# A weight's sign through an activation's slope, in an attention and two-MLP kernel with float64 weights

## The chip, the cores and the metric

The kernel runs on one core of a Trainium2 chip. The metric is the device time of one execution in microseconds (us). A difference under 0.2% is not told from none here.

## The reference, cut to what matters

```python
# q, k, v: [2, 12, 448, 64] float32; moe_w_in, moe2_w_in: [768, 2048], moe_w_out, moe2_w_out: [2048, 768], float64
scores = np.where(mask, -1e9, (q @ k.T) / 8)          # causal, per batch and head
attn = exp(scores - max); attn /= attn.sum(-1) + 1e-9
x = attn @ v                                          # reshaped to [896, 768]
h = np.maximum(x @ w_in, 0);  x = (h * h) @ w_out     # first MLP
h = x @ w_in2;  return (h - np.tanh(h)) @ w_out2      # second MLP
```

The weights are drawn in float32 and divided by a double, so they arrive as float64. The kernel takes them as pairs of 32-bit words and makes float32 of them on the chip.

## The kernel before, in words

**Three matmuls for one product.** Each MLP product is summed from three matmuls (lines 372 to 374): high part times high part, high times low, low times high. So every weight block and every activation is split into a high part, rounded by ScalarE, and a low part, the difference that VectorE takes.

**A weight unit and its passes.** The four weight matrices make 64 units (`NU`) of 128 x 768 weights. A unit is loaded by SyncE into one of three buffers `raw` (`w_load`, line 98). Then `w_prep` (lines 108 to 141) makes floats of it, with passes over 768 columns:

- `w_exp` on ScalarE (line 105): the upper word, read as float32, is scaled by 2^-112, which moves the exponent of a double to that of a float.
- `shift` on VectorE (line 115): the lower word is shifted right by 29.
- `merge` on VectorE (line 120): upper word shifted left by 3, or lower word. This drops the sign.
- `sign` on VectorE (line 125): the upper word's sign bit is put into the result.
- the conversion on ScalarE (line 127), the high part of the unit in a ring of 8 buffers `w`.
- `split` on VectorE (lines 134, 136): the low part. It frees the unit's `raw` buffer, into which unit u+3 is then loaded.

**Who sets the order.** The order on each engine is the order in which the code is written; no scheduler moves it. The VectorE passes stand in a list `todo` (lines 158 to 164): shift of unit u, split of unit u-1, merge of u, sign of u. `one()` takes the next pass while a budget lasts; each pass costs its price in `w_prep`, and each stage adds a share to the budget (`SHARE_PAIR` and the others, lines 37 to 40). The ScalarE passes are put into a second list, `act_late`, and are issued at the next call of `late()`, which the loop, `merge`, `split` and `need` make (`need` is called ahead of each MLP matmul group).

**Attention.** The loop over s has 14 stages for 12 pairs of heads. Stage s computes the scores of pair s, the exponentials of s and s-1, and the transposes and value product of pair s-2. In each stage ScalarE copies four transposed banks out of PSUM (`tcopy`, line 331), two ahead of the score maxima of the second half and two behind. From stage 8 on TensorE also runs one group of the first MLP's first product per stage (`fill`), ScalarE applies relu (line 487), square (493) and rounding (382) to it, and VectorE takes its low part (385) at the start of the next stage. From stage 2 to 7 a stage takes one pass from `todo`; from stage 8 on it takes three ahead of the second score maxima and what the budget leaves behind them.

**The MLPs.** After the loop TensorE runs the two MLPs in halves, with the remaining units prepared beside it.

Of the kernel before, what the change touches and what calls it, by code (L numbers as in the profile page):

```python
# [14 lines left out]
AF = mybir.ActivationFunctionType  # L15
ALU = mybir.AluOpType
# [17 lines left out]

SHARE_PAIR = (800, 3300)
SHARE_LAST = 3300
SHARE_HIDDEN = (2400, 500)
SHARE_OUT = 4000  # L40

EARLY = 6

# [21 lines left out]
def body(ctx: ExitStack, tc: tile.TileContext, qT, kT, vL, w1, w2, w3, w4, out):  # L65
    nc = tc.nc
# [24 lines left out]
    def words(u):  # L91
        v = raws[u].bitcast(I32).rearrange("p (n two) -> p n two", two=2)
        return v[:, :, 0], v[:, :, 1]

    def w_load(u):
        if u < NU:
            raws[u] = sb.tile([P, UC], I64, tag="raw", bufs=3, name=f"raw{u}")
            nc.sync.dma_start(out=raws[u], in_=units[u])

    def w_exp(u):  # L100


        if u < NU:
            h = words(u)[1].bitcast(F32)
            nc.scalar.activation(h, h, AF.Copy, scale=2.0**-112)  # L105

    def w_prep(u):

        st = {}

        def shift():
            if u == 0:
                act_late.append(lambda: w_exp(0))
            st["lo"], st["hi"] = lo, hi = words(u)
            nc.vector.tensor_scalar(out=lo, in0=lo, scalar1=29, scalar2=None, op0=ALU.logical_shift_right)

        def merge():
            late()
            lo, hi = st["lo"], st["hi"]
            nc.vector.scalar_tensor_tensor(out=lo, in0=hi, scalar=3, in1=lo, op0=ALU.logical_shift_left, op1=ALU.bitwise_or)  # L120
            act_late.append(lambda: w_exp(u + 1))

        def sign():
            lo, hi = st["lo"], st["hi"]
            nc.vector.scalar_tensor_tensor(out=lo, in0=hi, scalar=-0x80000000, in1=lo, op0=ALU.bitwise_and, op1=ALU.bitwise_or)  # L125
            st["w"] = ring(u)
            act_late.append(lambda: nc.scalar.copy(out=st["w"][:, 0], in_=lo.bitcast(F32)))  # L127

        def split():

            late()
            w, f = st["w"], st["lo"].bitcast(F32)
            if u % 2:
                nc.vector.scalar_tensor_tensor(out=w[:, 1], in0=w[:, 0].bitcast(F32), scalar=-(1.0 - 2.0**-24), in1=f, op0=ALU.mult, op1=ALU.add)  # L134
            else:
                nc.vector.tensor_sub(out=w[:, 1], in0=f, in1=w[:, 0])  # L136
            parts[u] = w
            raws.pop(u)
            w_load(u + 3)

        return [(shift, 470), (merge, 870), (sign, 870), (split, 870)]

    act_late = []
    budget = [0]
# [4 lines left out]
    def ring(u):  # L149
        taken.append(u)  # L150
        return sb.tile([P, 2, UC], F32R, tag="w", bufs=RING, name=f"w{u}")
# [6 lines left out]
    todo = []  # L158
    last = []
    for u in range(NU):  # L160
        shift, merge, sign, split = w_prep(u)
        todo += [(*shift, u, False), *last, (*merge, u, False), (*sign, u, True)]
        last = [(*split, u, False)]
    todo += last

    def late():
        while act_late:
            act_late.pop(0)()
# [120 lines left out]
    def blocks(n, t):  # L289
        return [c for cs in step(n, t) for c in cs]  # L290
# [162 lines left out]
    def first(l, half, m, b):  # L453

        u = (2 * l + half) * 2 * HALF + m
        dst = gdst(l, half, m, b)
        h = hbank(f"h{u}_{b}")
        for _ in first_pieces(l, half, m, b, h):
            pass
        if b == 1:  # L460
            freed[0] = u + 1
        return lambda: (act1, act2)[l](h, dst)
# [38 lines left out]
    def second(l, half, m, b):  # L501
        u0 = (2 * l + half) * 2 * HALF + HALF
        o = hbank(f"o{u0}_{m}_{b}")
        group(o, lambda k: (u0 + (m * HALF + k) // UNIT, (m * HALF + k) % UNIT), HALF, lambda k: g[k, b])
        if b == 1:
            freed[0] = u0 + (m + 1) * HALF // UNIT
        if half == 0:
            if b == 0 and m % 3 == 0:
                t = sb.tile([P, 3, B, S], F32, tag=f"v{m // 3}", name=f"part{l}_{m}")
                for i in range(3):  # L510
                    part[m + i] = t[:, i]
            nc.scalar.copy(out=part[m][:, b], in_=o)
        else:
            p = part[m][:, b]
            if l == 0:
                nc.vector.tensor_add(out=p, in0=o, in1=p)
                if b == 0:
                    x[m] = sb.tile([P, 2, B, S], F32R, tag=f"x{m}", name=f"y{m}")
                hi_of((x[m][:, 0, b], x[m][:, 1, b]), p)
                late()  # L520
                one()
                lo_of((x[m][:, 0, b], x[m][:, 1, b]), p)
            else:

                cuts = 2 if (m, b) == (KD - 1, B - 1) else 1
                w = S // cuts
                for i in range(cuts):
                    c = slice(i * w, i * w + w)
                    nc.vector.tensor_add(out=p[:, c], in0=o[:, c], in1=p[:, c])
                    (nc.scalar if i < cuts - 1 else nc.sync).dma_start(out=out[m * P : m * P + P, b * S + i * w : b * S + i * w + w], in_=p[:, c])  # L530
# [3 lines left out]
    for s in range(NPAIR + 2):  # L534
# [3 lines left out]
        if ss:  # L538
            budget[0] = min(budget[0], 0) + (SHARE_PAIR[f] if s > 1 else 0)
            e0, e1 = blocks(s, 0)[::-1], blocks(s, 1)  # L540
        else:
            budget[0] = min(budget[0], 0) + SHARE_LAST
        if sp:
# [73 lines left out]
    for l in range(2):  # L617
        for half in range(2):
# [3 lines left out]
            for m, b in order:  # L622
                budget[0] = min(budget[0], 0) + (SHARE_HIDDEN[l] if l == 1 or m < HALF - 1 else 0)
                first(l, half, m, b)()
                pump()
            flush()
            for m in range(KD):
                for b in range(B):
                    budget[0] = min(budget[0], 0) + SHARE_OUT
                    second(l, half, m, b)  # L630
# [39 lines left out]
```

## Time and profile before

| what | value |
|---|---|
| median of 3 runs (559.53 to 559.81) | 559.62 us |
| span of the profiled execution, first to last instruction | 558.0 us |
| granted TensorE clock, mean | 0.997 |
| TensorE matmuls busy | 550.9 us (99%), x3134 |
| VectorE busy | 403.7 us (72%), x727 |
| ScalarE busy | 336.6 us (60%), x650 |
| HBM read and written | 58.59 MB and 2.75 MB |

The page gives the span of the profiled execution and no time around it; the median lies 1.62 us above that span. Engines are named PE (TensorE matmul), PEld (its weight load), DVE (VectorE), ACT (ScalarE), POOL (GpSimd), SP (SyncE). Busy time counts a matmul from its start to a modelled end, so an engine shown as busy may still wait between matmuls.

### The profile page before, as it was taken

The page shows a single profiled execution, that of the slowest core. Times are in us where ns is not written, and L with a number is a line of the kernel's source. Part 1 is how long each engine was busy: PE and PEld are TensorE (multiplying, and loading weights), DVE is VectorE, ACT ScalarE, POOL GpSimd, SP SyncE. Part 2 cuts the span into 40 slices and gives each one's busy share as a digit, 9 for nine tenths or more (in the row PEclk, how much of TensorE's full clock was granted, in tenths as well). Part 3 has the DMA queues.
Part 4 walks back from the last instruction along what each step waited for, and adds up shares of the span by engine and source line. Part 5 has one row for each costly group of instructions (what it writes and reads, how often), then busy time and mean ns, then how long its engine had stood idle before and what let it go on. Part 6 is the DMA issues. An engine that isn't in the chain of part 4 may idle for free.

```text
span 558.0 us, 8044 instructions
## 1 busy us (share of the span) xinstructions
PE 550.9 (99%) x3134; PEld 482.4 (86%) x3134; DVE 403.7 (72%) x727; ACT 336.6 (60%) x650; POOL 1.8 (0%) x11
## 2 busy tenths in 40 slices
PE   7999999999999999999999999999999999999997
PEld 3666776899999999999999999999999999999996
DVE  5899998688574346564758599998887599988611
ACT  4999998777443347765334287876555587864100
POOL 1000000000000000000000000000000000000000
PEclk9899999999999999999999999999999999999999
DMA  8743421345253234222315130111666301015211
GB/s 275 253 156 107 141 64 58 125 158 168 78 178 123 80 116 156 89 97 107 115 57 167 61 113 1 56 58 56 195 205 202 124 11 57 1 56 186 84 49 49
DMA packets 15525, 61.85 MB, mean 111 GB/s; under 512 B 1664, under 2 KB 6400, under 8 KB 15488
## 3 DMA queue, kind: packets, MB, share of 16 engines
q1 hardware_dynamic: 15200, 61.00, 33.1%
q8 instruction: 24, 0.39, 0.3%
q10 hardware_dynamic: 288, 0.34, 0.2%
q14 instruction: 13, 0.11, 0.1%
HBM read 58.59 MB, written 2.75 MB: 110 GB/s over the span
## 4 chain that ended last, share of the span: by engine, by line
PE 84%; DVE 12%; ACT 2%; DMA 1%; issue 0%; DVEq 0%; ACTq 0%
PE o L372 14%; PE o L373 14%; PE o L374 14%; PE h L372 13%; PE h L374 13%; PE h L373 13%; DVE st L298 4%; DVE p L319 3%; ACT p L307 1%; PE o L343 1%; PE t L325 1%; DVE raw L120 1%; DVE x L360 1%; DMA k<-kT 1%; DVE st L300 1%; PE s L278 1%
## 5 line engine op out<-in xcount | busy, mean ns | idle before, releaser
L372 PE MATMUL o<-g,w 128*128 128x448 f32 x384 | 140.4, 366 | 0.0
L373 PE MATMUL o<-g,w 128*128 128x448 f32 x384 | 140.4, 366 | 0.0
L374 PE MATMUL o<-g,w 128*128 128x448 f32 x384 | 140.1, 365 | 0.0
L372 PEld LDWEIGHTS o<-g,w 128*128 128x128 f32 x384 | 72.1, 188 | 6.1
L374 PEld LDWEIGHTS o<-g,w 128*128 128x128 f32 x384 | 72.1, 188 | 6.0
L373 PEld LDWEIGHTS o<-g,w 128*128 128x128 f32 x384 | 72.1, 188 | 5.8
L127 ACT CAST w<-raw 128x768 fp32r<-128x768 f32 x64 | 58.0, 906 | 30.7 <-DVE raw L125 30.6
L105 ACT ACTIVATE raw<-raw 128x768 f32<-128x768 f32 x64 | 59.2, 924 | 23.6 <-DMA raw<-w 23.6
L372 PE MATMUL h<-x,w 128*128 128x448 f32 x192 | 72.7, 379 | 0.0
L374 PE MATMUL h<-y,w 128*128 128x448 f32 x192 | 70.6, 368 | 0.0
L373 PE MATMUL h<-y,w 128*128 128x448 f32 x192 | 70.6, 367 | 0.0
L372 PE MATMUL h<-y,w 128*128 128x448 f32 x192 | 70.6, 367 | 0.0
L373 PE MATMUL h<-x,w 128*128 128x448 f32 x192 | 70.5, 367 | 0.0
L374 PE MATMUL h<-x,w 128*128 128x448 f32 x192 | 70.5, 367 | 0.0
L125 DVE SCALAR_TENSOR_TENSOR raw<-raw 128x768 int32<-128x768 int32 x64 | 61.2, 957 | 1.2
L120 DVE SCALAR_TENSOR_TENSOR raw<-raw 128x768 int32<-128x768 int32 x64 | 61.0, 953 | 0.0
L136 DVE TENSOR_TENSOR w<-raw,w 128x768 fp32r<-128x768 f32 x32 | 30.6, 957 | 31.2 <-ACT w L127 31.0
L307 ACT ACTIVATE p<-s,st 128x128 f32<-128x128 f32 (+6 forms) x84 | 39.7, 485 | 9.2 <-DVE st L300 9.2
L134 DVE SCALAR_TENSOR_TENSOR w<-w,raw 128x768 fp32r<-128x768 f32 x32 | 30.6, 958 | 18.5 <-ACT w L127 18.5
L385 DVE TENSOR_TENSOR g<-r,g 128x448 fp32r<-128x448 f32 x32 | 20.0, 624 | 31.0 <-ACT g L382 30.9
L372 PEld LDWEIGHTS h<-x,w 128*128 128x128 f32 x192 | 36.0, 188 | 4.1
L374 PEld LDWEIGHTS h<-y,w 128*128 128x128 f32 x192 | 36.0, 188 | 3.4
(59 smaller groups left out, 744.7 us busy)
## 6 DMA issues: line engine op xcount, KB each, us to landing
raw<-w SPq DMA_DIRECT2D x64, 768.0 KB, 4.3
q<-qT SPq DMA_DIRECT2D x12, 224.0 KB, 4.8
k<-kT SPq DMA_DIRECT2D x11, 224.0 KB, 3.8
out<-part SPq DMA_DIRECT2D x11, 224.0 KB, 1.9
v<-vL SPq DMA_DIRECT2D x2, 1152.0 KB, 6.8
vend<-vL SPq DMA_DIRECT2D x1, 384.0 KB, 10.0
k<-kT ACTq DMA_DIRECT2D x1, 224.0 KB, 3.6
out<-part ACTq DMA_DIRECT2D x1, 112.0 KB, 1.7
```

The costliest lines, as they stand in the source:

```text
L105: nc.scalar.activation(h, h, AF.Copy, scale=2.0**-112)
L120: nc.vector.scalar_tensor_tensor(out=lo, in0=hi, scalar=3, in1=lo, op0=ALU.logical_shift_left, op1=ALU.bitwise_or)
L125: nc.vector.scalar_tensor_tensor(out=lo, in0=hi, scalar=-0x80000000, in1=lo, op0=ALU.bitwise_and, op1=ALU.bitwise_or)
L127: act_late.append(lambda: nc.scalar.copy(out=st["w"][:, 0], in_=lo.bitcast(F32)))
L134: nc.vector.scalar_tensor_tensor(out=w[:, 1], in0=w[:, 0].bitcast(F32), scalar=-(1.0 - 2.0**-24), in1=f, op0=ALU.mult, op1=ALU.add)
L136: nc.vector.tensor_sub(out=w[:, 1], in0=f, in1=w[:, 0])
L298: nc.vector.tensor_reduce(out=st[:, 0, SI[c] : SI[c] + 1], in_=sc[n, c], axis=AX.X, op=ALU.max, negate=True)
L307: nc.scalar.activation(prob[n % 3][:, POFF[c] : POFF[c] + w], sc.pop((n, c)), AF.Exp, bias=st[:, 0, i : i + 1], scale=0.125, accum_out=st[ ...
L372: nc.tensor.matmul(h, lhsT=hi, rhs=xh, start=(k == 0), stop=False)
L373: nc.tensor.matmul(h, lhsT=hi, rhs=xl, start=False, stop=False)
L374: nc.tensor.matmul(h, lhsT=lo, rhs=xh, start=False, stop=(k == kk - 1))
L385: nc.vector.tensor_sub(out=dst[1], in0=v, in1=dst[0])
```

## The change

ScalarE's pass on the upper word becomes a parametric relu: a word that is not negative is scaled by 2^-112 as before, a negative one by 2^-112 times 2^32. The 32 that this adds to the exponent field is bit 28 of the word, and `merge` shifts it to bit 31, the sign's place. VectorE's `sign` is gone. The conversion of unit u is now queued by `merge` and stands ahead of `w_exp` of unit u+1. The shares are scaled by about 0.72, the new sum of a unit's prices over the old.

```diff
-SHARE_PAIR = (800, 3300)
-SHARE_LAST = 3300
-SHARE_HIDDEN = (2400, 500)
-SHARE_OUT = 4000
+SHARE_PAIR = (575, 2370)
+SHARE_LAST = 2370
+SHARE_HIDDEN = (1725, 360)
+SHARE_OUT = 2870
...
-            nc.scalar.activation(h, h, AF.Copy, scale=2.0**-112)
+            nc.scalar.activation(h, h, AF.Prelu, scale=2.0**-112, alpha=2.0**32)
...
             nc.vector.scalar_tensor_tensor(out=lo, in0=hi, scalar=3, in1=lo, op0=ALU.logical_shift_left, op1=ALU.bitwise_or)
-            act_late.append(lambda: w_exp(u + 1))
-
-        def sign():
-            lo, hi = st["lo"], st["hi"]
-            nc.vector.scalar_tensor_tensor(out=lo, in0=hi, scalar=-0x80000000, in1=lo, op0=ALU.bitwise_and, op1=ALU.bitwise_or)
             st["w"] = ring(u)
             act_late.append(lambda: nc.scalar.copy(out=st["w"][:, 0], in_=lo.bitcast(F32)))
+            act_late.append(lambda: w_exp(u + 1))
...
-        return [(shift, 470), (merge, 870), (sign, 870), (split, 870)]
+        return [(shift, 470), (merge, 870), (split, 870)]
...
-        todo += [(*shift, u, False), *last, (*merge, u, False), (*sign, u, True)]
+        todo += [(*shift, u, False), *last, (*merge, u, True)]
```

TensorE's own order is the same in both, and ScalarE's has one table load in both, ahead of the first exponential. In the changed kernel the lines behind `w_prep` have numbers lower by 4, and lines 127, 134 and 136 are 122, 130 and 132. Names carry the number of the pair or unit: st9 is the statistics of pair 9, raw3 and w3 belong to unit 3.

ScalarE in stage 9, from the exponential of 384 columns to the rounding of the MLP group, before:

```order
L307 ACTIVATE p0_122,st9_981<-s9_0_1_941,st9_981 128x384
L105 ACTIVATE raw4_870<-raw4_870 128x768
L331 COPY pt7_967<-t7_2_1016 128x512
L331 COPY pt7_967<-t7_3_1022 128x512
L307 ACTIVATE p0_122,st9_981<-s9_0_0_940,st9_981 128x448
L487 ACTIVATE r_1035<-h1_0_958 128x448
L307 ACTIVATE p0_122,st9_981<-s9_1_0_998,st9_981 128x256
L307 ACTIVATE p0_122,st9_981<-s9_1_0_998,st9_981 128x192
L307 ACTIVATE p0_122,st9_981<-s9_1_1_999,st9_981 128x320
L493 ACTIVATE r_1035<-r_1035 128x448
L382 CAST g0_0_0_0_830<-r_1035 128x448
L127 CAST w3_1049<-raw3_706 128x768
```

and now:

```order
L303 ACTIVATE p0_122,st9_978<-s9_0_1_938,st9_978 128x384
L122 CAST w3_995<-raw3_613 128x768
L105 ACTIVATE raw4_861<-raw4_861 128x768
L327 COPY pt7_964<-t7_2_1015 128x512
L327 COPY pt7_964<-t7_3_1021 128x512
L303 ACTIVATE p0_122,st9_978<-s9_0_0_937,st9_978 128x448
L483 ACTIVATE r_1034<-h1_0_955 128x448
L303 ACTIVATE p0_122,st9_978<-s9_1_0_996,st9_978 128x256
L303 ACTIVATE p0_122,st9_978<-s9_1_0_996,st9_978 128x192
L303 ACTIVATE p0_122,st9_978<-s9_1_1_997,st9_978 128x320
L489 ACTIVATE r_1034<-r_1034 128x448
L378 CAST g0_0_0_0_830<-r_1034 128x448
```

The conversion of unit 3 has moved from behind the rounding to a place ahead of the last two bank copies. Stages 8, 10 and 11 show the same, with units 2, 4 and 5.

VectorE from the low part at the head of stage 10 to the second score maxima of that stage, before:

```order
L385 TENSOR_TENSOR g0_0_0_0_830<-r_1035,g0_0_0_0_830 128x448
L115 TENSOR_SCALAR raw4_870<-raw4_870 128x768
L298 TENSOR_REDUCE st10_1103<-s10_0_1_1062 128x1 x2
L298 TENSOR_REDUCE st10_1103<-s10_0_0_1061 128x1
L300 TENSOR_SCALAR st10_1103<-st10_1103 128x3
L360 TENSOR_TENSOR x1_68<-o7_1050,x1_68 128x448
L134 SCALAR_TENSOR_TENSOR w3_1049<-w3_1049,raw3_706 128x768
L311 TENSOR_SCALAR st9_981<-st9_981 128x7
L312 RECIPROCAL st9_981<-st9_981 128x7
```

and now:

```order
L381 TENSOR_TENSOR g0_0_0_0_830<-r_1034,g0_0_0_0_830 128x448
L130 SCALAR_TENSOR_TENSOR w3_995<-w3_995,raw3_613 128x768
L294 TENSOR_REDUCE st10_1102<-s10_0_1_1059 128x1 x2
L294 TENSOR_REDUCE st10_1102<-s10_0_0_1058 128x1
L296 TENSOR_SCALAR st10_1102<-st10_1102 128x3
L356 TENSOR_TENSOR x1_68<-o7_1048,x1_68 128x448
L120 SCALAR_TENSOR_TENSOR raw4_861<-raw4_861 128x768
L307 TENSOR_SCALAR st9_978<-st9_978 128x7
L308 RECIPROCAL st9_978<-st9_978 128x7
```

The merge of unit 4 stands where the split of unit 3 stood, and the split where the shift stood. Stage 11 has the same order with units 4 and 5. In stage 9 the merge of unit 3 stands behind three more normalisations, at the place that it had before; in stage 8 the merge of unit 2 takes that place, where the split of unit 1 stood before.

## Rows read from the trace of the kernel before

**Rows 1.** Windows: stretch and length, busy us (instructions) per engine, granted clock, DMA.
```profile
70.23:79.88 9.65, 9.65 (x88) 7.21 (x86) 9.02 (x25) 8.84 (x25) 0.00 (x0) 1.00 0.26 79
107.00:554.50 447.50, 447.50 (x2193) 411.18 (x2191) 309.81 (x447) 244.07 (x387) 0.00 (x0) 1.00 0.31 101
```
**Rows 2.** Timeline of PE, first scores of stages 3, 6, 7, 8: start us, us.
```profile
20.27 0.59 PE L278 MATMUL s<-k,q 64*64 64x448 f32 x2
...
38.75 0.62 PE L278 MATMUL s<-k,q 64*64 64x448 f32 x2
...
44.62 0.59 PE L278 MATMUL s<-k,q 64*64 64x448 f32 x2
...
50.96 0.59 PE L278 MATMUL s<-k,q 64*64 64x448 f32 x2
```
**Rows 3.** Timeline of PE, a value product of stage 9 and transposes of stage 12.
```profile
68.47 1.84 PE L343 MATMUL o<-pt,v 128*64 128x448 f32 x12
...
93.93 1.14 PE L325 MATMUL t<-ident,p 128*128 128x128 f32 x8 [0.25 <-ACT pt L331]
```
**Rows 4.** Timeline of DVE, stages 8 to 11; in brackets idle time before, and its releaser.
```profile
57.29 0.95 DVE L134 SCALAR_TENSOR_TENSOR w<-w,raw 128x768 fp32r<-128x768 f32 x1
...
62.69 0.61 DVE L385 TENSOR_TENSOR g<-r,g 128x448 fp32r<-128x448 f32 x1
...
67.44 0.95 DVE L120 SCALAR_TENSOR_TENSOR raw<-raw 128x768 int32<-128x768 int32 x1
...
69.99 0.95 DVE L125 SCALAR_TENSOR_TENSOR raw<-raw 128x768 int32<-128x768 int32 x1
...
72.39 0.63 DVE L385 TENSOR_TENSOR g<-r,g 128x448 fp32r<-128x448 f32 x1 [0.49 <-ACT g L382]
...
75.26 0.95 DVE L134 SCALAR_TENSOR_TENSOR w<-w,raw 128x768 fp32r<-128x768 f32 x1
...
82.11 0.62 DVE L385 TENSOR_TENSOR g<-r,g 128x448 fp32r<-128x448 f32 x1 [0.50 <-ACT g L382]
```
**Rows 5.** Timeline of ACT, stage 9, and the conversion in stage 11 with its follower.
```profile
66.36 0.93 ACT L105 ACTIVATE raw<-raw 128x768 f32<-128x768 f32 x1
67.17 1.06 ACT L331 COPY pt<-t 128x512 f32<-128x512 f32 x2
68.12 0.65 ACT L307 ACTIVATE p<-s,st 128x448 f32<-128x448 f32 x1
...
68.74 0.55 ACT L487 ACTIVATE r<-h 128x448 f32<-128x448 f32 x1
69.82 0.47 ACT L307 ACTIVATE p<-s,st 128x256 f32<-128x256 f32 x1 [0.53 <-DVE st L300]
...
71.18 0.58 ACT L493 ACTIVATE r<-r 128x448 f32<-128x448 f32 x1
71.79 0.57 ACT L382 CAST g<-r 128x448 fp32r<-128x448 f32 x1
...
91.71 0.90 ACT L127 CAST w<-raw 128x768 fp32r<-128x768 f32 x1
92.51 0.36 ACT L307 ACTIVATE p<-s,st 128x128 f32<-128x128 f32 x1
```
**Rows 6.** Lines by form: line, engine, operation, shapes, count, busy us, mean ns, idle before.
```profile
L125 DVE SCALAR_TENSOR_TENSOR raw<-raw 128x768 int32<-128x768 int32 x64 | 61.2, 957 | 1.2
...
L115 DVE TENSOR_SCALAR raw<-raw 128x768 int32<-128x768 int32 x64 | 35.5, 555 | 0.0
...
L105 ACT ACTIVATE raw<-raw 128x768 f32<-128x768 f32 x64 | 59.2, 924 | 23.6 <-DMA raw<-w 23.6
L127 ACT CAST w<-raw 128x768 fp32r<-128x768 f32 x64 | 58.0, 906 | 30.7 <-DVE raw L125 30.6
...
L412 ACT ACTIVATE w<-u,abias 128x448 f32<-128x448 f32 x32 | 21.5, 671 | 1.0
```
**Rows 7.** Lines by form of ACT, the one table load.
```profile
L225 ACT ACT_TABLE_LOAD x1 | 1.3, 1283 | 1.2 <-PEq L663 1.2
```

More of the change, by code (lines that the diff above doesn't have):

```diff
@@ L160, in body @@
     for u in range(NU):
-        shift, merge, sign, split = w_prep(u)
-        todo += [(*shift, u, False), *last, (*merge, u, False), (*sign, u, True)]
+        shift, merge, split = w_prep(u)
+        todo += [(*shift, u, False), *last, (*merge, u, True)]
         last = [(*split, u, False)]
```

## The prediction

> **What bounds the kernel now.** I read the windows first, then the timelines of the three engines that hand work to each other in the attention stages, then the lines by form for the price of a pass. From 107.00 to 554.50 us TensorE is busy for the whole 447.5 us at full clock while VectorE works 309.8 us of it [rows 1]. There VectorE and ScalarE have room, and a pass less on VectorE moves nothing. So the change can act on the time only before 107 us, in the attention stages.
>
> There the reader should compare three clocks. **TensorE:** the stages without MLP work start at 20.27, 38.75, 44.62 and 50.96 us for stages 3, 6, 7 and 8 [rows 2]. The shortest of them, stage 6, takes 44.62 - 38.75 = 5.87 us. Five of these would take 29.35, and the five from 20.27 to 50.96 took 30.69, so TensorE loses 1.34 us there to waits. From stage 8 on a stage takes 9.65 us with TensorE busy throughout [rows 1]. **VectorE and ScalarE:** they go round a loop of nearly the same length. The low part of the MLP group (L385) starts at 62.69, 72.39 and 82.11 us, that is every 9.70 and 9.72 us, and each time VectorE has waited about 0.5 us for ScalarE's rounding [rows 4]. So in stages 9 to 11 two things are nearly tied: TensorE's own work, 9.65 us, and the loop from the low part through the score maxima, the exponentials, square and rounding back to the next low part, 9.7 us. A stage becomes longer as soon as that loop does.
>
> The pass that is removed, `sign`, stands at 69.99 us in stage 9 [rows 4]. That is behind the maxima for which ScalarE waited until 69.82 [rows 5], and VectorE still has to wait before 72.39. In these stages the sign pass lies in the shadow of ScalarE; it is not on the loop.
>
> **The change, part by part.**
>
> *The sign pass.* 64 passes of 0.957 us, 61.2 us of VectorE's time [rows 6]. All but the first nine or so run beside a TensorE that is never idle [rows 1]: nothing. Of the early ones, those of stages 8 to 11 lie in the shadow named above: nothing, as long as ScalarE closes the loop. What cover there is, is that wait of 0.5 us, and it grows below. Those of units 0 and 1 stand in stages 4 and 8. The places move up there, so that up to the merge of stage 8 VectorE has the passes shift 1, split 0, merge 1, shift 2, split 1 instead of sign 0, shift 1, split 0, merge 1, sign 1, shift 2: a pass of 0.957 less. Against it, ScalarE gets two passes in a row (a conversion and the next unit's exponent pass) in front of the exponentials of stages 4 and 7, 1.6 us by the price below, on which scores and VectorE's low part of x wait. I set the two against each other and let VectorE reach the place of the merge in stage 8 at 57.29 us as before [rows 4]; the bounds are 0.96 earlier and 0.7 (1.6 less 0.96, rounded up) later.
>
> *The slope.* The same 768 columns in place. The exponent pass takes 0.924 and the conversion 0.906 [rows 6]; the dearest activation with an extra operand takes 0.671 for 448 columns [rows 6], 1.15 for 768 if scaled. The bounds are 0.906 and 1.15; I take 0.924, since it is the same instruction with the same shape, 0.81 from its start to the next one's start (66.36 to 67.17) [rows 5].
>
> *The conversion's new place.* This is the term that decides. In stages 8 to 11 the conversion of the unit just merged now stands between the 384-column exponential and the last two bank copies, together with the exponent pass. That is a longer piece of ScalarE work there, and a wait: the conversion reads what `merge` writes, so ScalarE stands still until VectorE's merge is done. Before, only the exponent pass stood there, which needs no merge and ran at 66.36, while VectorE began the merge at 67.44 [rows 4, 5]. Behind the waiting conversion are queued: the exponent pass, two bank copies (for TensorE's value product, which started at 68.47 [rows 3]), the 448-column exponential, relu, three exponentials, square and rounding. VectorE's next low part waits for the rounding.
>
> The length of that ScalarE piece, start to start [rows 4, 5]: conversion 0.81 (taken as the exponent pass's), exponent pass 0.81, two copies 67.17 to 68.12 = 0.95, exponential 68.12 to 68.74 = 0.62, relu 0.55, three exponentials 69.82 to 71.18 = 1.36, square 71.18 to 71.79 = 0.61, rounding up to VectorE's start 71.79 to 72.39 = 0.60. The sum is **6.31 us**. The hand from VectorE to ScalarE costs 0.03.
>
> - Stage 8: merge at 57.29, done at 58.24, conversion at 58.27, the low part of stage 9 at 64.58: 1.89 late against 62.69 [rows 4].
> - Stage 9: from low part to merge 67.44 - 62.69 = 4.75, the order between is as before; merge 0.95, hand 0.03, ScalarE 6.31: a round of 12.04 instead of 9.70. Late by 4.23.
> - Stage 10: the merge stands where the split stood, 75.26 - 72.39 = 2.87 after the low part [rows 4], plus 0.40 since a split (0.957, as every pass of this form) stands where a shift of 0.555 stood [rows 6]: 3.27. With 0.95, 0.03 and 6.31 the round is 10.56 instead of 9.72. Late by 5.07.
> - Stage 11: the same order, late by 5.91.
>
> Then 0.80 comes back: the conversion that stood behind the rounding in stage 11 (91.71 to 92.51) [rows 5] is no longer ahead of the exponential and the bank copies for which TensorE waited at 93.93 [rows 3]. From there the order gives TensorE no other waiting than before, and it is full to the end. So 5.91 - 0.80 = **5.1 us** stay. TensorE shows them as waits ahead of the value products of stages 9 to 11 and the transposes of stage 12. The 1.34 us of earlier waits are not gained, because stage 12 starts by the loop and not by TensorE.
>
> *DMA.* The load of unit 3 is issued one stage earlier on SyncE's queue, ahead of the q of pair 9 and the k of pair 8; these are needed at stage 9 and 8, many us later. I cost it at nothing; were the k late, stage 8 would start late, and it is inside the bound of 0.7.
>
> *Shares.* They keep the passes at about the same place per unit; after 107 us it costs nothing.
>
> The sum is made against the profiled span of 558.0 us: 563.1. The median of the runs is 1.62 above that span, so I add 5.1 to 559.62: **564.7 us**.
>
> **The rivals.**
>
> *One turn only* (0.12). If stages 10 and 11 fall back to TensorE's 9.65, because VectorE's passes overlap more than I count, only 1.89 + 2.34 - 0.80 = 3.4 us stay: 563.0. For it: the merge is early in those stages. Against it: the round of 10.56 has no slack in the rows.
>
> *TensorE stays the bound: faster* (0.13). If the conversion never has to wait for the merge, ScalarE has nothing more to do per stage than before, and TensorE could run its stages back to back: 1.34 us gained, 558.3 us. It decides in favour of this if VectorE is more than 2 us ahead of today's place, so that the merge of stage 9 ends at 66.36 instead of 68.39, when ScalarE is free. For it: VectorE has a pass less per unit. Against it: VectorE cannot run ahead past the low part, which waits for ScalarE's rounding already now [rows 4].
>
> *Hidden anyway* (0.10). The longer piece in mid-stage is made up by the earlier start of the next stage's copies, and gains and losses cancel: 559.6 us.
>
> *The slope is dearer or not the same function set* (0.05). One table load is 1.283 us [rows 7], and the order of the changed kernel holds only that one. If the pass itself took twice the 0.924, the loop would get 0.92 more in four rounds, 3.7 us: 568.4. The Trainium skill ("ScalarE activation tables: per-element evaluation and per-set limits", What a function is on this engine) says that with the same operands an instruction costs the same whichever table it reads, and that functions of two sets are one table load apart. By its first half this rival falls away and the sum stays; by its second a set without the slope would put loads around every such pass. No row before shows this function.
>
> **How the numbers follow.** The forecast has 0.60, the rivals 0.12, 0.13, 0.10 and 0.05. The forecast's own range: relu may overlap its follower as the exponent pass does, 0.93 - 0.81 = 0.12 in each of four rounds (-0.5) [rows 5], and with -0.96 at stage 8's start this gives 563.3; +0.7 and a pass of 1.15 in four rounds (+0.9) give 566.3. The range that holds 8 in 10 takes in these, the one-turn case and the case of no change, and leaves out the faster and the dearest: 559.4 to 566.3. What 0.2% is, 1.1 us, is about what a measurement can tell from no change. Slower by more: 0.60 + 0.12 + 0.05 = 0.77. Within: 0.10. Faster: 0.13.
>
> **What would show it.** In the changed profile, right: the low part L381 of stages 9 to 11 comes every 12 and 10.5 us; ScalarE's conversions L122 there wait for VectorE's L120; VectorE's wait for the rounding grows from 0.5 to over 2 us; TensorE idles about 2 us in stage 9 and 0.8 in 10 and 11; the table load stays one. The forecast is wrong if the low parts keep their pitch of 9.7 us, if the conversions there wait for nothing, or if the time after the loop changes.

## The result, and the profile of the changed kernel

The changed kernel takes 564.40 us (median of 4 runs, 564.12 to 564.56), the kernel before, run beside it, 559.67 (559.53 to 559.81): a ratio of 1.0087, 95% interval 1.0074 to 1.0099, or 4.7 us slower. The forecast was 564.7. The profiled execution has a span of 562.8 us against 558.0, 4.8 more. Engines over the span, from the profile's first part:

```profile
PE 552.0 (98%) x3134; PEld 481.3 (86%) x3134; DVE 345.6 (61%) x663; ACT 333.9 (59%) x650; POOL 1.8 (0%) x11
```

VectorE has 64 instructions and 58 us less, and the kernel is slower: the engine's busy share was no guide. Two groups of the lines by form of ScalarE, the slope and the conversion, and a window behind the attention stages (columns as in rows 6 and 1):

```profile
L105 ACT ACTIVATE raw<-raw 128x768 f32<-128x768 f32 x64 | 59.2, 925 | 0.0
L122 ACT CAST w<-raw 128x768 fp32r<-128x768 f32 x64 | 57.8, 904 | 32.2 <-DVE raw L120 32.2
```
```profile
107.00:559.00 452.00, 452.00 (x2222) 414.33 (x2221) 258.80 (x392) 245.33 (x393) 0.00 (x0) 1.00 0.31 102
```

The slope costs what the scaling cost [rows 6], and from 107 us TensorE is busy throughout at full clock as before [rows 1]. So the time went ahead of that. The timeline of VectorE, merges (L120) and low parts (L381) of stages 8 to 12, to be laid beside [rows 4]:

```profile
57.38 0.95 DVE L120 SCALAR_TENSOR_TENSOR raw<-raw 128x768 int32<-128x768 int32 x1
...
64.54 0.62 DVE L381 TENSOR_TENSOR g<-r,g 128x448 fp32r<-128x448 f32 x1 [3.56 <-ACT g L378]
...
69.30 0.95 DVE L120 SCALAR_TENSOR_TENSOR raw<-raw 128x768 int32<-128x768 int32 x1
...
76.44 0.62 DVE L381 TENSOR_TENSOR g<-r,g 128x448 fp32r<-128x448 f32 x1 [3.08 <-ACT g L378]
...
79.71 0.95 DVE L120 SCALAR_TENSOR_TENSOR raw<-raw 128x768 int32<-128x768 int32 x1
...
86.92 0.62 DVE L381 TENSOR_TENSOR g<-r,g 128x448 fp32r<-128x448 f32 x1 [2.12 <-ACT g L378]
...
97.38 0.62 DVE L381 TENSOR_TENSOR g<-r,g 128x448 fp32r<-128x448 f32 x1 [2.10 <-ACT g L378]
```

The low part of stage 12 in the kernel before:

```profile
91.84 0.63 DVE L385 TENSOR_TENSOR g<-r,g 128x448 fp32r<-128x448 f32 x1 [0.50 <-ACT g L382]
```

The low parts come after 11.90, 10.48 and 10.46 us instead of 9.70 and 9.72, and VectorE's wait for the rounding (L378) has grown from 0.5 to between 2.1 and 3.6. What the rounding was late for stands in the timeline of ScalarE, stage 9 and the conversion of stage 10, against [rows 5]:

```profile
67.31 0.57 ACT L303 ACTIVATE p<-s,st 128x384 f32<-128x384 f32 x1
...
70.29 0.88 ACT L122 CAST w<-raw 128x768 fp32r<-128x768 f32 x1 [2.32 <-DVE raw L120]
71.08 0.88 ACT L105 ACTIVATE raw<-raw 128x768 f32<-128x768 f32 x1
71.86 1.05 ACT L327 COPY pt<-t 128x512 f32<-128x512 f32 x2
72.81 0.64 ACT L303 ACTIVATE p<-s,st 128x448 f32<-128x448 f32 x1
...
75.84 0.56 ACT L378 CAST g<-r 128x448 fp32r<-128x448 f32 x1
...
80.70 0.90 ACT L122 CAST w<-raw 128x768 fp32r<-128x768 f32 x1 [0.42 <-DVE raw L120]
```

ScalarE is free at 70.29 - 2.32 = 67.97, stands still for 2.32 us until VectorE's merge of 69.30 is done, and only then come the exponent pass and the bank copies, which could have run. The copies started at 67.17 before. TensorE waits for those copies; its timeline, first scores of stages 3 and 8, the value product of stage 9, and its waits up to the transposes of stage 12; below them, the last part of that value product in the kernel before:

```profile
19.94 0.59 PE L274 MATMUL s<-k,q 64*64 64x448 f32 x2
...
52.33 0.59 PE L274 MATMUL s<-k,q 64*64 64x448 f32 x1
...
69.84 0.97 PE L339 MATMUL o<-pt,v 128*64 128x448 f32 x4
72.48 1.08 PE L339 MATMUL o<-pt,v 128*64 128x320 f32 x8 [1.67 <-ACT pt L327]
73.49 0.27 PE L339 MATMUL o<-pt,vend 64*64 64x64 f32 x2
...
82.97 1.08 PE L339 MATMUL o<-pt,v 128*64 128x320 f32 x8 [0.63 <-ACT pt L327]
...
93.42 1.08 PE L339 MATMUL o<-pt,v 128*64 128x320 f32 x8 [0.58 <-ACT pt L327]
...
94.97 0.47 PE L368 MATMUL h<-x,w 128*128 128x448 f32 x1 [0.20 <-ACT r L483]
...
98.67 1.14 PE L321 MATMUL t<-ident,p 128*128 128x128 f32 x8
```
```profile
70.23 0.27 PE L343 MATMUL o<-pt,vend 64*64 64x64 f32 x2
```

These waits are 3.1 us. Before stage 8, from 19.94 to 52.33, the five stages take 32.39 us against 30.69 [rows 2], 1.7 more; since stage 3 starts 0.33 earlier than before, stage 8 starts 1.37 late. The transposes of stage 12 start at 98.67 instead of 93.93 [rows 3]: 4.74 of the 4.8 us are lost by then, 1.37 ahead of stage 8 and 3.37 behind its start. That is more than the waits alone, 3.1 less the old 0.25 [rows 3]. An interrupted value product loses more than the idle time in brackets: that of stage 9 takes 73.49 - 69.84 = 3.65 us up to its last part instead of 70.23 - 68.47 = 1.76 [rows 3], 1.89 more around a wait of 1.67.

### The profile page after: what moved, and what is told of

Read it like the earlier page. It is cut to its first block, busy times and chain, and to the rows that moved or that the text cites. A ratio compares the mean times of both kernels' runs of the same rounds, so it can differ in the third digit from the quotient of the medians.

```text
span 562.8 us, 8014 instructions
## 1 busy us (share of the span) xinstructions
PE 552.0 (98%) x3134; PEld 481.3 (86%) x3134; DVE 345.6 (61%) x663; ACT 333.9 (59%) x650; POOL 1.8 (0%) x11
## 4 chain that ended last, share of the span: by engine, by line
PE 83%; DVE 8%; ACT 7%; issue 1%; DMA 1%; DVEq 0%; ACTq 0%
PE o L368 14%; PE o L369 14%; PE o L370 14%; PE h L368 13%; PE h L370 13%; PE h L369 13%; ACT p L303 3%; DVE st L294 3%; DVE p L315 2%; ACT pt L327 1%; ACT raw L105 1%; PE t L321 1%; DVE x L356 1%; PE o L339 1%; DMA k<-kT 1%
## 5 line engine op out<-in xcount | busy, mean ns | idle before, releaser
L120 DVE SCALAR_TENSOR_TENSOR raw<-raw 128x768 int32<-128x768 int32 x64 | 61.0, 953 | 0.0
L381 DVE TENSOR_TENSOR g<-r,g 128x448 fp32r<-128x448 f32 x32 | 20.0, 625 | 57.5 <-ACT g L378 57.5
L132 DVE TENSOR_TENSOR w<-raw,w 128x768 fp32r<-128x768 f32 x32 | 30.6, 957 | 36.6 <-ACT w L122 36.4
L508 ACT COPY part<-o 128x448 f32<-128x448 f32 x24 | 12.8, 534 | 58.2 <-PE o L370 58.2
L130 DVE SCALAR_TENSOR_TENSOR w<-w,raw 128x768 fp32r<-128x768 f32 x32 | 30.6, 956 | 25.3 <-ACT w L122 25.2
L115 DVE TENSOR_SCALAR raw<-raw 128x768 int32<-128x768 int32 x64 | 35.6, 557 | 5.6 <-DMA raw<-w 5.4
```

The lines of the kernel that those rows point to most:

```text
L381: nc.vector.tensor_sub(out=dst[1], in0=v, in1=dst[0])
```

## The experiments

The theory is the forecast's: the conversion waits on ScalarE for the merge, with everything behind it. The rivals: the slope is dearer; the missing pass or the new order on VectorE harms; the longer ScalarE piece harms without any wait. "Burst" below is the conversion and the next exponent pass in a row on ScalarE, ahead of the exponentials of stages 4 and 7; a "round" is the time from one low part to the next. Line numbers in the views are those of each run's own kernel. "Held" is this edit of the changed kernel, with `release()`, which issues what is held, called ahead of a split and at a place further back in each stage:

```diff
-            act_late.append(lambda: nc.scalar.copy(out=st["w"][:, 0], in_=lo.bitcast(F32)))
+            (held if holding[0] else act_late).append(lambda: nc.scalar.copy(out=st["w"][:, 0], in_=lo.bitcast(F32)))
```

**The slope alone.** The kernel before, `sign` kept, with one line of the change:

```diff
-            nc.scalar.activation(h, h, AF.Copy, scale=2.0**-112)
+            nc.scalar.activation(h, h, AF.Prelu, scale=2.0**-112, alpha=2.0**32)
```


> The kernel before with the parametric relu in place of the scaling, all else kept: the sign pass still runs and finds the sign already there. Theory (the conversion's new place makes the loss, the slope costs nothing): 559.6 us, the low parts at the heads of stages 9 to 12 every 9.7 us, the exponent pass 0.92 us. Rival (the slope is dearer on ScalarE): with 0.9 us more per pass, about 563 us.

Measured: 559.32 us, ratio 0.9999 (0.9989 to 1.0008). The pass takes 928 ns, the low parts keep their pitch of 9.72. The slope costs nothing. The Trainium skill ("ScalarE activation tables: per-element evaluation and per-set limits", What a function is on this engine) says that the table does not change an instruction's cost; 925 and 928 beside 924 ns agree.

**The pass gone, everything else in its old place.** Order and shares of before with the slope; the step `sign` stays in the list and issues only the conversion, behind the rounding:

```diff
         def sign():
-            nc.vector.scalar_tensor_tensor(out=lo, in0=hi, scalar=-0x80000000, in1=lo, op0=ALU.bitwise_and, op1=ALU.bitwise_or)
             st["w"] = ring(u)
```


> The kernel before with the slope, and the sign step left in the list of passes with its price but issuing nothing on VectorE, so that every other pass, the conversion's place behind the rounding too, stays where it was. Theory: the removal itself is harmless and gains at most the 1.34 us that TensorE waits in stages 3 to 7; 558.9 us, between 558.3 and 559.6, low parts every 9.65 to 9.7 us. Rival (taking VectorE's pass away or the slope makes the loss): 562 us or more.

Measured: 558.88 us, 0.9991 (0.9982 to 1.0001). Low parts at 61.40, 71.21, 80.94 and 90.66; VectorE's wait for the rounding, in stage 10, is 1.36 instead of 0.49 us. The removed pass turned into waiting, as [rows 4] let expect. Taking it out does no harm; the loss is in what else the change moves.

**The conversion behind the rounding in stages 8 to 11.** Held, issued behind `squares()`:

```diff
+        holding[0] = 8 <= s < NPAIR
...
         squares()
+        release()
```


> The changed kernel, with the conversion held back in stages 8 to 11 until behind the rounding of the MLP group, its place before. Passes, shares and the two passes in a row in stages 3 and 6 stay as changed. Theory: the rounds of stages 9 to 11 fall from 11.9 and 10.5 us to about 9.7, and what is left is TensorE's late start of stage 8 (about 1.4 us): 560.8 us, between 560.3 and 561.3. Rival (the passes in a row ahead of stages 4 and 7, or the new order of VectorE's passes, make the loss): it stays at 564.4 us.

Measured: 560.84 us, 1.0026 (1.0016 to 1.0036); low parts every 9.72, 9.98 and 10.00 us. What is left of the loss lies in the five early stages: from first scores at 19.84 to first scores at 52.19 they take 32.35 us, 30.69 before [rows 2]. The timeline of TensorE has two waits there, in stages 4 and 7:

```profile
29.09 0.76 PE L282 MATMUL s<-k,q 64*64 64x320 f32 x8 [0.48 <-ACT p L311]
...
48.42 0.76 PE L282 MATMUL s<-k,q 64*64 64x320 f32 x8 [0.32 <-ACT p L311]
```

There the conversion and the next unit's exponent pass stand in a row ahead of exponentials, for whose score banks TensorE waits.

**The conversion behind relu.** As above, but `release()` follows `relus()`: ahead of the three exponentials, square and rounding.

> The changed kernel, with the conversion held back in stages 8 to 11 until behind relu, still ahead of the three exponentials: the wait for the merge is covered by the bank copies, but ScalarE's piece up to the rounding stays as long. Theory (wait and length both count, the wait 2.3 us in stage 9 and 0.5 in 10 and 11): rounds of about 9.7, 10.0, 10.0 us, 561.4 us. If the wait alone counts: as with the conversion behind the rounding, 560.8 us. If the length alone counts: near 563 us.

Measured: 560.72 us, 1.0023 (1.0013 to 1.0032); low parts every 9.72, 9.93 and 9.91. The main expectation, that the conversion's length counts in this place, missed by 0.7: the same time as behind the rounding. Without the wait, 0.8 us more on ScalarE here finds cover.

**Longer piece, no wait.** The kernel before with an extra ScalarE pass over 768 columns of a scratch tile, which waits for nobody, ahead of the last two bank copies of stages 8 to 11:

```diff
...
+        if f and ss:
+            nc.scalar.activation(extra, extra, AF.Copy, scale=1.0)
```


> The kernel before, with one more ScalarE pass of 768 columns on a scratch tile ahead of the last two bank copies in stages 8 to 11: the piece of ScalarE work there gets as long as in the changed kernel, and waits for nothing. Nothing is left out. Theory (the wait for the merge decides, the length fits into idle time of 0.5 to 0.85 us ahead of the three exponentials): 559.7 us, at most 0.3 us in one stage. Rival (the length of the piece decides): four times 0.81, 562.8 us.

Measured: 559.31 us, 0.9999 (0.9989 to 1.0008). Four passes of 862 ns, and nothing is lost. The rival of the mere length falls. Behind a wait the length does count: in stage 10 of the changed kernel ScalarE stands still for only 0.42 us (80.70 above), but the round is 10.48 - 9.72 = 0.76 longer, about the 0.8 us of the conversion.

**Held everywhere.** `holding[0] = s < NPAIR`, issued behind `squares()`: no wait ahead of the copies, no two passes in a row.

> The changed kernel, with the conversion held back until behind the squares of its own or the next stage in all attention stages, so that stages 4 and 7 too no longer find a conversion and an exponent pass in a row ahead of their exponentials. Against the run that held it in stages 8 to 11 alone (560.84 us), this undoes the burst and nothing else. Theory (the burst is the remaining 1.4 us): 559.4 us, stage 8 of TensorE about 30.6 us behind stage 3 instead of 32.35. Rival (the remaining loss is VectorE's split that follows the low part and waits for the conversion in stages 10 and 11, 0.3 us each, or the new order): 560.4 us or more.

Measured: 559.41 us, 1.0002 (0.9993 to 1.0011). The whole loss is gone with the change's own list, shares and slope in place. The way there is not quite the expected one: stage 8 starts 51.07 - 19.87 = 31.20 us behind stage 3 and not 30.6, and the low parts come every 9.72, 9.99 and 10.02 us.

**Held up to stage 7 only.** `holding[0] = s < 8`: the wait is there, the burst not.

> The change with the conversion held behind the rounding's place up to stage 7 only; in stages 8 to 11 it stands ahead of the bank copies, as in the change. If the two parts of the loss simply add, 564.4 - 1.4 = 563.0 us. If the burst ahead of stages 4 and 7 only fills time that VectorE's merge in stage 8 would be waited for anyway, 564.4. Without the burst the merge of stage 8 should then come about 1 us earlier than 57.38, and the rounds from low part to low part stay 11.9, 10.5 and 10.5 us.

Measured: 563.95 us, 1.0084 (1.0067 to 1.0101). The merge of stage 8 came 0.84 us earlier than in the change, yet the gain is 0.45, too small for these intervals; the time lies between the 563.0 and the 564.4 that were expected. Timelines of VectorE and TensorE, and two windows:

```profile
56.54 0.95 DVE L120 SCALAR_TENSOR_TENSOR raw<-raw 128x768 int32<-128x768 int32 x1
```
```profile
71.63 1.08 PE L347 MATMUL o<-pt,v 128*64 128x320 f32 x8 [2.02 <-ACT pt L335]
...
72.81 1.56 PE L282 MATMUL s<-k,q 64*64 64x448 f32 x8
```
```profile
72.60:75.00 2.40, 2.40 (x24) 1.54 (x23) 0.00 (x0) 2.37 (x10) 0.00 (x0) 0.57 0.00 0
75.00:77.00 2.00, 2.00 (x12) 1.81 (x11) 1.42 (x3) 1.66 (x5) 0.00 (x0) 0.66 0.00 0
```

By the medians the waiting place of the conversion alone is worth 563.95 - 559.41 = 4.5 us, the burst alone 560.84 - 559.41 = 1.4, both together 564.40 - 559.41 = 5.0. By the intervals each of these differences is uncertain by more than half a microsecond, so that 5.9 against 5.0 decides nothing. The profiled executions are closer to each other: in the four kernels stage 3 starts between 19.84 and 19.98 us. The transposes of stage 12 in them, with everything held, with the burst alone, with the waiting place alone, and with both:

```profile
93.88 1.14 PE L329 MATMUL t<-ident,p 128*128 128x128 f32 x8 [0.38 <-ACT pt L335]
```
```profile
94.95 1.14 PE L329 MATMUL t<-ident,p 128*128 128x128 f32 x8 [0.34 <-ACT pt L335]
```
```profile
97.78 1.14 PE L329 MATMUL t<-ident,p 128*128 128x128 f32 x8
```
```profile
98.67 1.14 PE L321 MATMUL t<-ident,p 128*128 128x128 f32 x8
```

That is 1.07 us for the burst, 3.90 for the waiting place and 4.79 for both: there the two prices add within 0.2 us. Without the burst the merge of stage 8 and each low part behind it come 0.84 to 0.88 us earlier, and the rounds stay as in the change. TensorE is 69.84 - 68.63 = 1.21 us earlier at its value product of stage 9, so it waits longer there (2.02 us here, 1.67 in the change).

**The conversion on GpSimd.** The change with the conversions of units 0 to 5 on an idle engine:

```diff
-            act_late.append(lambda: nc.scalar.copy(out=st["w"][:, 0], in_=lo.bitcast(F32)))
+            if u < 6:
+                nc.gpsimd.tensor_copy(out=st["w"][:, 0], in_=lo.bitcast(F32))
+            else:
+                act_late.append(lambda: nc.scalar.copy(out=st["w"][:, 0], in_=lo.bitcast(F32)))
```


> The changed kernel, with the conversions of units 0 to 5, those of the attention stages, on GpSimd, which has nothing to do there; ScalarE keeps the exponent passes alone. Theory (ScalarE's wait for the merge and its two passes in a row make the whole loss): both are gone, so the low parts come every 9.65 to 9.75 us, stage 8 starts no later than before, and the time is 558.5 us, between 558.0 and 559.4. Rival (VectorE's new order of passes has a part in the loss): 560 us or more. If GpSimd's pass slows VectorE's or is longer than the 4 us that the split of unit 3 leaves it, the low parts will show it: over 560 us too, with VectorE waiting for w.

Measured: 559.92 us, 1.0008 (0.9999 to 1.0016). The loss is gone, but the time lies above the expected range, which ended at 559.4, and the low parts come every 9.72, 10.14 and 10.10 us. Stage 7 in the timelines: GpSimd's pass, VectorE's normalisations beside it and TensorE's transposes that wait for them; below them the same normalisations in the kernel with the conversion held everywhere.

```profile
45.62 0.95 POOL L123 CAST w<-raw 128x768 fp32r<-128x768 f32 x1 [18.45 <-DVE raw L120]
```
```profile
45.47 1.68 DVE L318 TENSOR_SCALAR p<-p,st 128x256 f32<-128x256 f32 x3
```
```profile
46.84 0.80 PE L324 MATMUL t<-ident,p 128*128 128x128 f32 x3 [0.54 <-DVE p L318]
```
```profile
45.65 1.04 DVE L323 TENSOR_SCALAR p<-p,st 128x256 f32<-128x256 f32 x3
```

Beside GpSimd's pass the three take 0.64 us more. The Trainium skill ("Perfetto Trace Analysis", Optimizing Scalar/DVE Operations) says that the two engines share a read port of SBUF, so that moving work from one to the other may not help; 1.68 against 1.04 us fits that, though no run here shows that the port is the reason.

**Conversions on VectorE, in the place of the sign passes.** The kernel with the pass gone and the old places, and in `sign`:

```diff
+            if u < 2:
+                nc.vector.tensor_copy(out=st["w"][:, 0], in_=lo.bitcast(F32))
```


> The order and shares of the kernel before with the slope and without the sign pass, and the conversions of units 0 and 1 on VectorE, in the places that the sign passes had. If ScalarE's early passes are what holds the stages from 3 to 8 above TensorE's own 5.87 us, the five stages take about 30.1 us instead of 30.6 and ScalarE's piece up to the first low part loses another 0.8 with the conversion of unit 1: up to 1 us less than the 558.9 of the kernel without the sign pass in the old places, so 557.9. If VectorE's copy only fills the place that the sign pass left, nothing is gained: 558.9 to 559.6.

Measured: 558.38 us, 0.9980 (0.9971 to 0.9989): 0.9 us below the kernel before, run beside it (559.27), which is no more than the 0.2% that is not told from none here, and short of the 557.9 expected. With `u < 6`:

> The same, with the conversions of units 0 to 5 on VectorE in the places of the sign passes. In stages 9 to 11 ScalarE then has 0.8 us less per stage, and the stages can come down from 9.72 to TensorE's own 9.65 at most: 557.7, another 0.2 us below the kernel with two. If VectorE's passes close the loop there instead, the low parts come later than every 9.72 us and the time goes above 558.9.

Measured: 558.36 us, 0.9982 (0.9973 to 0.9991): the further four bring nothing, and the 557.7 expected is not reached. With two, TensorE starts those stages every 9.65 us (first scores at 50.10, 59.74, 69.39 and 79.04), as it did before [rows 1], so there is nothing left to gain there. VectorE's timeline of the kernel with two:

```profile
31.99 0.55 DVE L127 CAST w<-raw 128x768 fp32r<-128x768 f32 x1
```

The copy takes 0.55 us there and 0.90 on ScalarE. The five stages up to stage 8 take 30.30 us (first scores at 19.80 and 50.10), against 30.59 with both on ScalarE: 0.3 us less, where 0.5 was expected.

**The change's own order with six conversions on VectorE.** The same lines in `merge`, directly behind it:

> The change as it is, its list and shares, with the conversions of units 0 to 5 on VectorE, directly behind the merge. ScalarE then waits for no merge and has no burst, so both parts of the loss go: 558.4 us, as with the old places, if VectorE's 0.55 us is covered. Since it stands ahead of the second maxima there and not behind them, it may lengthen the loop by up to 0.5 us in each of stages 8 to 11: then 559.0 to 560.4. If the loss came from the list's new order on VectorE and not from the wait, it stays above 563.

Measured: 560.85 us, 1.0027 (1.0017 to 1.0036), a little above the range for a lengthened loop. Its timelines of VectorE and TensorE:

```profile
62.19 0.63 DVE L384 TENSOR_TENSOR g<-r,g 128x448 fp32r<-128x448 f32 x1 [1.36 <-ACT g L381]
...
67.94 0.56 DVE L123 CAST w<-raw 128x768 fp32r<-128x768 f32 x1
...
72.51 0.63 DVE L384 TENSOR_TENSOR g<-r,g 128x448 fp32r<-128x448 f32 x1 [0.90 <-ACT g L381]
```
```profile
94.44 1.14 PE L324 MATMUL t<-ident,p 128*128 128x128 f32 x8 [0.31 <-ACT pt L330]
```

Low parts come every 10.3 us, 0.6 above 9.72: ahead of the second maxima the copy is in the loop, behind them (the run before, every 9.72) it is not. TensorE starts stages 8 to 11 every 9.65 us all the same (first scores at 51.20, 60.85, 70.50 and 80.14) and waits for the loop only at the transposes of stage 12. The wait before the low part, 0.9 to 1.4 us, is no spare time of the loop: the rounding it waits for stands behind exponentials for which ScalarE waits on VectorE's maxima, as ScalarE's timeline shows:

```profile
69.94 0.47 ACT L306 ACTIVATE p<-s,st 128x256 f32<-128x256 f32 x1 [0.52 <-DVE st L299]
```

## Why the prediction was right

- *The sign pass: nothing.* Right. With it gone and all else in place the time is the same within 0.2%, and the wait behind it grew by 0.87 us, from 0.49 to 1.36. One reading was too wide: that VectorE waits each time holds at 72.39 and 82.11, but [rows 4] show no wait at 62.69, so the sign pass of stage 8 was not in the shadow. With the pass gone the low part of stage 9 came 61.40 - 50.42 = 10.98 us behind the first scores of stage 8 instead of 62.69 - 50.96 = 11.73. In the time this stays below 0.2%, and in the changed kernel that low part goes by the merge.
- *The slope: 0.924.* Right: 0.925, and alone 0.9999.
- *The start of stage 8.* The forecast set a pass less on VectorE against two passes in a row on ScalarE and took 57.29; it was 57.38. Without the burst the merge comes at 56.54, 0.75 earlier than the forecast's place, inside its bound of 0.96; the burst then costs it 0.84. That the two cancel was assumed and not worked out, and in part it was luck: with the forecast's own 1.6 for the burst the merge would have come 0.64 late.
- *The ScalarE piece, 6.31.* From the conversion of stage 9 to the low part it took 76.44 - 70.29 = 6.15. The forecast counted relu with its whole duration and named the overlap as a reason for less; the next exponential did start 0.42 after relu's start at 73.43.
- *The rounds.* 12.04, 10.56 and 10.56 were forecast; 11.90, 10.48 and 10.46 came, in all 0.3 less, nearly all of it the piece, which was shorter by 0.16, 0.09 and 0.10. From low part to merge 4.75 and 3.27 were forecast; 69.30 - 64.54 = 4.76 and 79.71 - 76.44 = 3.27 came.
- *What comes back.* The low part of stage 12 is 97.38 - 91.84 = 5.54 us late, the transposes of stage 12 are 4.74 late: the forecast 0.80 came back there. After 107 us nothing changes.
- *DMA: nothing.* Right: the timeline of TensorE from stage 3 to 107 us shows no wait for a transfer.
- *TensorE's waits.* 1.67, 0.63 and 0.58 came where about 2 and 0.8 were named. The five early stages became 1.7 us longer, which the forecast did not price for TensorE; it did not have to, since the loop, which TensorE meets in stage 9, goes by the merge.
- *The rivals.* One turn only: the rounds of stages 10 and 11 did stay above 9.65. TensorE as the bound: it would need conversions that never wait; held everywhere they do not, and the time is then 559.4, no gain: the five early stages, in which ScalarE has the same passes, then take 51.07 - 19.87 = 31.2 us, not 29.35. Hidden anyway, and a dearer slope: shown wrong by the result and by the slope alone.

## What to carry to other kernels

A pass that is taken off an engine in the shadow of another is worth nothing, but what moves up behind it can cost. On an engine that works in order, ask of each moved instruction what it waits for and what stands behind it: a pass of the same length without a wait cost nothing in that place, the conversion waiting there for another engine cost 3.9 us over four stages (4.5 by the medians). If two causes may act on one start time, take each away alone and both together; here their prices added within 0.2 us in the profiled executions, while medians taken beside different repeats were too coarse to tell.

## What the runs showed of the hardware that was not expected

- A 128x768 conversion to the matmul's type takes 0.55 us on VectorE, 0.90 on ScalarE and 0.88 to 0.95 on GpSimd.
- A GpSimd pass of 0.95 us lengthened three VectorE normalisations beside it from 1.04 to 1.68 us. Beside VectorE's maxima it cost nothing: in the same run four maxima that start at 67.96, beside GpSimd's pass of 68.10 to 68.98, take 1.27 us, as in the kernel with the conversion held everywhere.
- In the profiled execution of the kernel held up to stage 7, after TensorE's idle 2.02 us, the granted clock was 0.57 and 0.66 from 72.60 to 77.00 us, so in part at the lower level of 1.2 GHz, and a group of eight score matmuls took 1.56 us where 0.91 is usual. After the change's 1.67 us at the same place it stayed at 1.00 (its window below, columns as in rows 1). It cost nothing that the loop shows: the low parts of that run came every 11.89, 10.46 and 10.46 us, as in the change.

```profile
72.60:75.00 2.40, 2.40 (x30) 1.43 (x31) 0.76 (x3) 2.40 (x9) 0.00 (x0) 1.00 0.00 0
```
